# Moving the stores of one layer to the scalar engine's queue, and reordering the work at the border between two layers

## The chip, the cores and the metric

The kernel runs on one NeuronCore of a Trainium2 chip. The core has a matrix engine (PE; its weight loads are listed as PEld), a vector engine (DVE), a scalar engine (ACT), GpSimd (POOL) and a sync engine (SP) that here does nothing but issue DMAs. The metric is the device time of one execution in microseconds. The kernel before takes 1653.34 us, the median of three runs from 1653.21 to 1654.24.

## The reference

Attention within chunks of 64 positions feeds a two-layer chain of feed-forward blocks. Inputs are 64-bit floats that the kernel converts itself.

```python
scores = scale * np.matmul(q_c, k_c.transpose(0, 1, 2, 4, 3))        # 8 x 8 heads, 576 positions, chunks of 64
attn   = softmax(scores);  out = np.matmul(attn, v_c)
x  = out.transpose(0, 2, 1, 3).reshape(4608, 512)
h1 = x @ w_in1;  g1 = np.maximum(h1, 0) + alpha * np.minimum(h1, 0);  y = g1 @ w_out1     # 512 -> 2048 -> 512
h2 = y @ w_in2;  g2 = h2 - np.tanh(h2);                               out = g2 @ w_out2
```

## The kernel before

Each float32 operand of a large product is split into two parts, `hi` and `lo` (`hi` is the value rounded to a shorter mantissa, `lo` the rest), and a product is three matmuls: hi by hi, lo by hi, hi by lo. The 4608 tokens are nine blocks of 512.

**Layer one, blocks 0 to 6.** `step_one` does one of 16 feed-forward slices of a block: `up` (12 matmuls into a bank `hps`), then the `down` of the slice two steps earlier (12 matmuls into four banks `y`), then `act_g` (ACT reads `hps` as `neg` and `g`). At the last slice of a block (or half block) `done()` empties the four `y` banks: `put_bank` copies a bank to a stage tile `yst` on ACT (L642) and issues its store to `ysc` or `half` (L643) on SP. There are three stage tiles (`neg` and `xst` take turns in the same three), so the fourth bank's copy waits until the first store has landed. The next block's `down` starts a bank at a time and needs that bank emptied. Attention runs beside it, a tile of 128 tokens at a time: loads of `raw` (32 small DMAs of q and k for a pair of tiles, L340), `att_a` (DVE transposes them into `qt` and `ktc`, L385), `att_s` (scores on PE, L400), and so on; for tiles of the last two blocks `att_x_out` copies the result to a stage tile `xst` and issues its store to `xsc` (L536) on SP.

**Parked weights.** Beside this, second-layer weights are formed and written back to DRAM. `park_load` fetches 64-bit words into `desk[0]` (`rw`), `park_form` converts them (`to_f32_a`: two ACT instructions, L115 and L118; `to_f32_b`: four DVE instructions) into `desk[2]` (`mr`), `park_split` writes `hi` into `desk[1]` (`whi`, ACT L254) and `lo` (POOL L255), `park_store` issues both stores (L266). For a piece of kind `d`, the words and later `lo` lie in the same half of `mr`.

**Pairs of blocks.** From `two_blocks` on, two blocks go through together with a seven-product scheme on sums and differences of their operands. Pair s=0 is layer one on blocks 7 and 8, pairs s=1 to 4 are layer two, and `small` does the ninth block. `cycle(s, p)` is one of eight rounds of a pair; it issues products p1, p5, p6, p2, p3, p7, p4 (six matmuls each, L1200) and in between, as `gaps` says, matmuls of the output side (`downs`, L1107). PE reads a bank that `copy` (ACT, L1210) or `add` (DVE, L1207) prepared: p6 needs `copy(H0, X)` done, p3 needs `add(H1, X, p5)` done. `border(s)` hangs the preparation of the next pair's operands on named places of the rounds: `tokens` is a difference of two blocks (DVE, L710), `put` splits one into hi (ACT, L698) and lo (DVE, L700). `on(s, p, place, ...)` puts a call behind that place of round p.

Each engine runs its instructions in the order in which they were written, whatever waits ahead of them; the program's order decides what stands in SP's queue before what. Every DMA also signals one of eight completion counters (`DMAHW0` to `DMAHW7`), which are given out in turn over all DMAs of the program; a DMA first waits until the one eight before it has landed.

Of the kernel before, what the change touches and what calls it, by code (L numbers as in the profile page):

```python
# [11 lines left out]
I32 = mybir.dt.int32  # L12
# [15 lines left out]
def kernel(  # L28
# [19 lines left out]
    nc = tc.nc  # L48
# [3 lines left out]
    P = 128  # L52
# [148 lines left out]
    def park_load(kind, n, c):  # L201
# [7 lines left out]
            )  # L209
        parked[kind, n, c] = raw  # L210

    def park_form(kind, n, c):

        if kind == "u1":
            mr = desk[1]
            quarters = mr[:, 0:4].rearrange("p (g e) m -> p g e m", e=2)
            for e in range(2):
                hi, lo = (
                    wsplit[2 * n + e, 0][:, i].bitcast(F32).rearrange("p (g c m) -> p g c m", g=2, c=2)[:, :, c]
                    for i in range(2)  # L220
                )
                nc.gpsimd.tensor_tensor(out=quarters[:, :, e], in0=hi, in1=lo, op=ALU.add)
            sums = ((3, 1, 3, ALU.add), (1, 0, 1, ALU.subtract), (0, 3, 0, ALU.subtract), (2, 2, 0, ALU.subtract))
        else:
            mr = desk[2]
            flat = mr.rearrange("p s m -> p (s m)")
            to_f32_b([to_f32_a(parked[kind, n, c], flat[:, :512], flat.bitcast(I32)[:, 512:])])
            sums = ((4, 1, 3, ALU.add), (1, 0, 1, ALU.subtract), (5, 4, 0, ALU.subtract), (6, 2, 5, ALU.subtract))
        for o, x, y, op in sums if kind != "d" else ():
            nc.gpsimd.tensor_tensor(out=mr[:, o], in0=mr[:, x], in1=mr[:, y], op=op)  # L230
        parked[kind, n, c] = mr

    def park_split(kind, n, c):
# [2 lines left out]
        hi = desk[1].bitcast(F32R)  # L236
        if kind == "d":
            wd2[n] = dram.tile([P, 2, 4, P], F32, name=f"wd2_{n}")
            m, h, lo = mr[:, 0:4], hi[:, 0:4], mr[:, 4:8]
            to = [wd2[n][:, i] for i in range(2)]  # L240
        else:
            layer = 0 if kind == "u1" else 1
            if (layer, n) not in wu:
                wu[layer, n] = dram.tile([P, 7, 2, 2, P], F32, name=f"wu{layer}_{n}")
            if layer == 0:
                m, h, lo = mr[:, 0:4], hi[:, 4:8], mr[:, 0:4]
                to = [wu[0, n][:, 0:4, i, c] for i in range(2)]
            else:
                m, h, lo = mr[:, 0:7], hi[:, 0:7], mr[:, 0:7]
                to = [wu[1, n][:, :, i, c] for i in range(2)]  # L250
# [277 lines left out]
    def att_x_out(t):  # L528
# [4 lines left out]
        nc.scalar.activation(  # L533
            out=st.rearrange("p h (c d) -> p c h d", c=2), in_=xps.pop(t), func=AF.Copy
        )
        nc.sync.dma_start(out=xsc[j].rearrange("kk p t -> p kk t")[:, :, o:o + P], in_=st)  # L536


    def up(f, x, n, cols=None, hp=None):
# [97 lines left out]
    def put_bank(a, to, last=False):  # L637
        st = stage.tile([P, 512], F32, tag="st", name="yst")
        if last:
            nc.vector.tensor_copy(st, a)  # L640
        else:
            nc.scalar.activation(out=st, in_=a, func=AF.Copy)  # L642
        nc.sync.dma_start(out=to, in_=st)  # L643

    def finish_half(j, acc):
        spill[j] = dram.tile([KD, P, NB], F32, name=f"half{j}")
# [511 lines left out]
    def two_blocks(queue):  # L1158
# [91 lines left out]
        def parks_done():  # L1250
            spare.append(tuple(wide.tile([P, 2, 512], F32R, tag="w", name="xo") for _ in range(2)))
            new_slots(wide.tile([P, 2, 512], F32, tag="r", name="slots", bufs=1))
            raw["e1"] = [att.tile([P, NB], F32, tag=tag, name="e1") for tag in ("p", "pt")]
            raw["e2"] = [vpool.tile([P, NB], F32, tag="v", name="e2") for _ in range(2)]

        def border(s):
            m = s + 1
            if s == 0:
                on(s, 5, "p1", load_y, m, "b11", "b12")
                on(s, 6, "p1", load_y, m, "b22", "b21")  # L1260
                on(s, 6, "end", parks_done)
                on(s, 6, "end", turn, m)
                for p, place, fn, args in (
                    (6, "end", put, ("p1", "b11", V)), (6, "end", tokens, ("b11", "b12", "b11", V)),
                    (6, "end", tokens, ("b12", "b22", "b12", V)),
                    (7, "p6", put, ("p5", "b11", V)), (7, "p6", tokens, ("e1", "b22", "b11", V)),
                    (7, "p7", put, ("p6", "e1", V)), (7, "p7", tokens, ("e2", "b21", "e1", V)),
                    (7, "p4", put, ("p2", "b21", V)), (7, "end", put, ("p3", "b22", V)),
                    (7, "end", put, ("p7", "b12", V)), (7, "end", put, ("p4", "e2", V)),
                ):  # L1270
                    on(s, p, place, fn, m, *args)
                on(s, 7, "p7", drop, "b11")
                on(s, 7, "end", drop, "b21", "b22", "b12")
                on(s, 7, "end", lambda: [raw.pop(name) for name in ("e1", "e2")])
                return
            on(s, 4, "p1", load_y, m, "b11", "b12")
# [5 lines left out]
            on(s, 6, "end", tokens, m, "e1", "b22", "b11", V)  # L1282
            on(s, 6, "end", tokens, m, "e2", "b21", "e1", V)
            for p, place, product_, name in (
                (7, "p1", "p5", "b11"), (7, "end", "p6", "e1"), (7, "end", "p2", "b21"), (7, "end", "p3", "b22"),
                (8, "p6", "p7", "b12"), (8, "p6", "p4", "e2"),
            ):
                on(s + p // 8, p % 8, place, put, m, product_, name, V)
# [11 lines left out]
        for i, f in enumerate(range(DP, KF)):  # L1300
            p, form, split, later, store, latest, load = slips[i % 3]
            p += 2 * (i // 3)
            on(0, p, form, park_form, "d", f, 0)
            on(0, p + later, split, park_split, "d", f, 0)
            on(0, p + latest, store, park_store, "d", f, 0)
# [180 lines left out]
```

## Time and profile before

| | |
|---|---|
| median of three runs | 1653.34 us |
| the profiled execution | 1653.51 us, of which the span is 1651.5 us |
| PE busy | 1608.0 us (97%), 9309 matmuls |
| DVE busy | 1218.6 us (74%) |
| ACT busy | 989.2 us (60%) |
| POOL busy | 452.0 us (27%) |
| mean granted clock of PE | 0.99 |

All times in the rows are microseconds from the start of the span. A line number such as L643 is a line of the kernel before. A busy share says little here: PE is busy nearly all the time, so the time is its matmuls plus the few places where it stands still, and those are listed one by one in the view of waits. PE's granted clock is 1.00 or 0.50 of full speed (2.4 and 1.2 GHz).

### The profile page before, as it was taken

The numbers are of one execution on the slowest core, as the hardware profiler recorded it, in microseconds if no ns is written. First come the engines' busy times: TensorE is split into PE (matmuls) and PEld (weight loads), VectorE is DVE, ScalarE is ACT, GpSimd is POOL, SyncE is SP. The second block draws the span as 40 slices with busy tenths as digits, with TensorE's granted clock in tenths as the row PEclk, the third lists the DMA queues.
The fourth block names the chain that finished last, engine by engine and source line by source line (L and its number), as shares of the span: only waits on it lengthen the run. The fifth ranks groups of instructions, "written<-read, shape, count | busy, mean of one in ns | idle before, by whom it ended". The sixth has DMA issues, their size and how long they took to land. (4 is left out here: it accounts for less than half of the span.)

```text
span 1651.5 us, 26382 instructions
## 1 busy us (share of the span) xinstructions
PE 1608.0 (97%) x9309; PEld 1326.2 (80%) x9309; DVE 1218.6 (74%) x1864; ACT 989.2 (60%) x1769; POOL 452.0 (27%) x418
## 2 busy tenths in 40 slices
PE   7899999989989999999999999999999999999999
PEld 6678878877878887887778888888888888888887
DVE  7868957766768786674578688868886988688663
ACT  5657544554545554666557576757675767576553
POOL 1000001424435344323222222222222232223334
PEclk9899999999999999999999999999999999999999
DMA  9551334564656666648768764655465546545650
GB/s 255 167 189 48 90 78 114 122 170 118 162 130 155 157 166 182 211 139 282 271 207 289 256 211 136 192 161 175 141 191 165 168 147 185 161 145 171 206 160 26
DMA packets 339299, 276.49 MB, mean 167 GB/s; under 512 B 180432, under 2 KB 244960, under 8 KB 339168
## 3 DMA queue, kind: packets, MB, share of 16 engines
q1 hardware_dynamic: 339168, 274.82, 55.7%
q8 instruction: 73, 1.20, 0.3%
q14 instruction: 58, 0.48, 0.1%
HBM read 192.95 MB, written 81.79 MB: 166 GB/s over the span
## 5 line engine op out<-in xcount | busy, mean ns | idle before, releaser
L578 POOL TENSOR_TENSOR glo<-arena,ghi 128x512 fp32r<-128x512 f32 x147 | 206.4, 1419 | 505.7 <-ACT ghi L575 355.2
L547 PE MATMUL hps<-x,w 128*128 128x512 f32 (+1 forms) x1356 | 331.6, 394 | 5.9 <-ACT kt L374 5.3
L547 PEld LDWEIGHTS hps<-x,w 128*128 128x128 f32 x1356 | 257.6, 192 | 60.3 <-ACT kt L374 5.8
L1107 PE MATMUL y<-w,ghi 128*128 128x512 f32 x1152 | 296.2, 389 | 0.0
L1107 PEld LDWEIGHTS y<-w,ghi 128*128 128x128 f32 x1152 | 214.7, 188 | 43.4
L617 PE MATMUL y<-ghi,w 128*128 128x512 f32 x880 | 233.8, 399 | 6.2 <-ACT yst L642 6.2
L1200 PE MATMUL hpb<-w,wu 128*128 128x512 f32 (+1 forms) x888 | 205.3, 374 | 5.5 <-DVE hpb L1207 4.8
L1200 PE MATMUL hps<-w,wu 128*128 128x512 f32 (+1 forms) x888 | 205.1, 375 | 1.5 <-ACT hpb L1210 1.4
L617 PEld LDWEIGHTS y<-ghi,w 128*128 128x128 f32 x880 | 163.5, 190 | 42.2 <-ACT yst L642 7.1
L1200 PEld LDWEIGHTS hpb<-w,wu 128*128 128x128 f32 x888 | 158.7, 189 | 37.9 <-DVE hpb L1207 6.5
L1200 PEld LDWEIGHTS hps<-w,wu 128*128 128x128 f32 x888 | 158.8, 189 | 34.7 <-ACT hpb L1210 4.8
L1107 PE MATMUL y<-w,glo 128*128 128x512 f32 x576 | 163.0, 389 | 0.0
L560 DVE SCALAR_TENSOR_TENSOR g<-neg,nalpha_sb,g 128x512 f32<-128x512 f32 x112 | 90.8, 811 | 78.6 <-ACT g L559 78.4
L558 ACT ACTIVATE neg<-hps 128x512 f32<-128x512 f32 x112 | 66.5, 594 | 116.5 <-PE hps L547 116.3
L617 PE MATMUL y<-glo,w 128*128 128x512 f32 x440 | 126.4, 390 | 0.0
L1107 PEld LDWEIGHTS y<-w,glo 128*128 128x128 f32 x576 | 107.7, 188 | 22.2
L578 DVE TENSOR_TENSOR glo<-g,ghi 128x512 fp32r<-128x512 f32 x111 | 93.9, 846 | 35.9 <-ACT ghi L575 34.8
L575 ACT ACTIVATE ghi<-g 128x512 fp32r<-128x512 f32 x112 | 70.7, 631 | 70.2 <-DVE g L560 70.0
L607 DVE SCALAR_TENSOR_TENSOR arena<-sq,arena 128x512 f32<-128x512 f32 x119 | 103.0, 865 | 4.1
L599 ACT ACTIVATE w<-sq,bias_sb 128x512 f32<-128x512 f32 x144 | 104.0, 723 | 0.0
L602 ACT ACTIVATE ktc<-sq,edge_sb 128x512 f32<-128x512 f32 x144 | 103.8, 721 | 0.0
L608 DVE COPY_PREDICATED arena<-ktc,th 128x512 f32<-128x512 uint32 x119 | 93.2, 783 | 10.5 <-ACT th L591 0.5
(179 smaller groups left out, 2431.3 us busy)
## 6 DMA issues: line engine op xcount, KB each, us to landing
wu<-wu SPq DMA_DIRECT2D x336, 256.0 KB, 3.3
g<-arena SPq DMA_DIRECT2D x66, 256.0 KB, 3.6
arena<-g SPq DMA_DIRECT2D x65, 256.0 KB, 3.8
raww<-in_moe_w_in_dram SPq DMA_DIRECT2D x16, 512.0 KB, 5.4
v<-in_v_dram SPq DMA_DIRECT2D x32, 256.0 KB, 3.9
raww<-in_moe_w_out_dram SPq DMA_DIRECT2D x16, 512.0 KB, 5.4
rw<-in_moe_w_in_dram SPq DMA_DIRECT2D x16, 512.0 KB, 5.5
wu<-whi SPq DMA_DIRECT2D x32, 256.0 KB, 2.9
```

The source lines that it names most:

```text
L547: nc.tensor.matmul(out=hp[:, cols], lhsT=w[:, a, m], rhs=x[b][:, kk, cols], start=(kk == 0 and i == 0), stop=(kk == KD - 1 and i == 2),)
L558: nc.scalar.activation(out=neg, in_=hp, func=AF.Relu, scale=-1.0)
L560: nc.vector.scalar_tensor_tensor(out=g, in0=neg, scalar=nalpha_sb[:, f:f + 1], in1=g, op0=ALU.mult, op1=ALU.add)
L575: nc.scalar.activation(out=hi, in_=g, func=AF.Copy)
L578: lo_engine.tensor_tensor(out=lo, in0=g, in1=hi.bitcast(F32), op=ALU.subtract)
L599: nc.scalar.activation(out=self.w, in_=self.sq, func=AF.Square, bias=bias_sb)
L602: nc.scalar.activation(out=self.mask, in_=self.sq, func=AF.Relu, bias=edge_sb)
L607: nc.vector.scalar_tensor_tensor(out=g, in0=self.sq, scalar=TS[0], in1=g, op0=ALU.add, op1=ALU.mult)
L608: nc.vector.copy_predicated(g, self.mask.bitcast(U32), self.th)
L617: nc.tensor.matmul(out=acc[t], lhsT=lhsT, rhs=rhs, start=(f == ends[0] and i == 0), stop=(f == ends[1] and i == 2))
L1107: nc.tensor.matmul(out=self.acc[t], lhsT=lhsT, rhs=rhs, start=(self.f == self.ends[0] and i == 0), stop=(self.f == self.ends[1] and i == 2),)
L1200: nc.tensor.matmul(out=o, lhsT=w[:, a, c], rhs=x[c][:, b, :h], start=start and i == 0 and c == 0, stop=i == 2 and c == 1, skip_group_check ...
```

## The change

Five edits. (1) The stores of `put_bank` and of `att_x_out` are issued by ACT instead of SP: 24 and 8 DMAs. (2) For three of the parked pieces of s=0 (those whose form stands at the end of rounds 0, 2 and 4) the two ACT instructions of `to_f32_a` move ahead, to the place `p4` of the same round. (3) `lo` of a `d` piece goes to the second half of `desk[1]` instead of the half of `mr` that held the words. (4) At the border of s=0 the differences come first and go to tiles of the attention (`extras`, three `tokens` at the end of round 6), and the tiles that the parked weights leave, the turn of the operand tiles and all seven `put` come later (from round 7's p6 to round 0 of the next pair). (5) At the borders of the other pairs the `put` of p5 moves from behind p1 of round 7 to behind p6.

```diff
+    def park_words(kind, n, c):
+        flat = desk[2].rearrange("p s m -> p (s m)")
+        parked[kind, n, c] = to_f32_a(parked[kind, n, c], flat[:, :512], flat.bitcast(I32)[:, 512:])
...
-            to_f32_b([to_f32_a(parked[kind, n, c], flat[:, :512], flat.bitcast(I32)[:, 512:])])
+            if not isinstance(parked[kind, n, c], tuple):
+                park_words(kind, n, c)
+            to_f32_b([parked[kind, n, c]])
...
-            m, h, lo = mr[:, 0:4], hi[:, 0:4], mr[:, 4:8]
+            m, h, lo = mr[:, 0:4], hi[:, 0:4], desk[1][:, 4:8]
...
-        nc.sync.dma_start(out=xsc[j].rearrange("kk p t -> p kk t")[:, :, o:o + P], in_=st)
+        nc.scalar.dma_start(out=xsc[j].rearrange("kk p t -> p kk t")[:, :, o:o + P], in_=st)
...
-        nc.sync.dma_start(out=to, in_=st)
+        nc.scalar.dma_start(out=to, in_=st)
...
+                on(s, 6, "p1", extras)
+                on(s, 6, "end", tokens, m, "e1", "b12", "b11", V)
+                on(s, 6, "end", tokens, m, "b12", "b22", "b12", V)
+                on(s, 6, "end", tokens, m, "e2", "b22", "e1", V)
+                on(s, 7, "p6", parks_done)
+                on(s, 7, "p6", turn, m)
                 for p, place, fn, args in (
-                    (6, "end", put, ("p1", "b11", V)), (6, "end", tokens, ("b11", "b12", "b11", V)),
-                    (6, "end", tokens, ("b12", "b22", "b12", V)),
-                    (7, "p6", put, ("p5", "b11", V)), (7, "p6", tokens, ("e1", "b22", "b11", V)),
-                    (7, "p7", put, ("p6", "e1", V)), (7, "p7", tokens, ("e2", "b21", "e1", V)),
+                    (7, "p6", put, ("p1", "b11", V)), (7, "p6", tokens, ("b11", "b21", "e2", V)),
+                    (7, "p7", put, ("p5", "e1", V)), (7, "p4", put, ("p6", "e2", V)),
                     (7, "p4", put, ("p2", "b21", V)), (7, "end", put, ("p3", "b22", V)),
-                    (7, "end", put, ("p7", "b12", V)), (7, "end", put, ("p4", "e2", V)),
+                    (8, "p6", put, ("p7", "b12", V)), (8, "p6", put, ("p4", "b11", V)),
...
-                (7, "p1", "p5", "b11"), (7, "end", "p6", "e1"), (7, "end", "p2", "b21"), (7, "end", "p3", "b22"),
+                (7, "p6", "p5", "b11"), (7, "end", "p6", "e1"), (7, "end", "p2", "b21"), (7, "end", "p3", "b22"),
...
+            if form == "end":
+                on(0, p, "p4", park_words, "d", f, 0)
```

Three places of the program's order follow, each before and after. The line numbers of the kernel after are 5 to 11 higher.

On SP, before, the four stores of block 2 (`ysc2`) stand behind raw loads, parked weights, a `v` load and a load of words. The name in the brackets is what the DMA waits for.

```order
L340 DMA raw_3410<-in_k_dram 32x8x32 [waits DMAHW4_49]
L266 DMA wu1_1_3617<-whi_2784 896x1x128 [waits DMAHW5_49,Activation_49]
L266 DMA wu1_1_3617<-mr_2785 896x1x128 [waits DMAHW6_49,DVE_49,Pool_49]
L301 DMA v_3625<-in_v_dram 128x8x64 [waits DMAHW7_49,PE_49]
L206 DMA rw_2783<-in_moe2_w_in_dram 128x2x256 [waits DMAHW0_49]
L643 DMA ysc2_3694<-yst_3695 128x512 [waits DMAHW1_49,Activation_49]
L643 DMA ysc2_3694<-yst_3698 128x512 [waits DMAHW2_49,Activation_49]
L643 DMA ysc2_3694<-yst_3701 128x512 [waits DMAHW3_49,Activation_49]
L643 DMA ysc2_3694<-yst_3704 128x512 [waits DMAHW4_49,Activation_49]
```

A store is issued only when all that stands above it has been issued. On ACT, after, the same four stores stand between the copies that fill their tiles.

```order
L647 ACTIVATE yst_3695<-y0_2668 128x512 [waits PE_49]
L648 DMA ysc2_3694<-yst_3695 128x512 [waits DMAHW1_49,Activation_49]
L647 ACTIVATE yst_3698<-y1_2669 128x512 [waits PE_49]
L648 DMA ysc2_3694<-yst_3698 128x512 [waits DMAHW2_49,Activation_49]
L647 ACTIVATE yst_3701<-y2_2670 128x512 [waits DVE_49,PE_49]
L648 DMA ysc2_3694<-yst_3701 128x512 [waits DMAHW3_49,Activation_49]
L647 ACTIVATE yst_3704<-y3_2671 128x512 [waits DMAHW1_49,PE_49]
L648 DMA ysc2_3694<-yst_3704 128x512 [waits DMAHW5_49,Activation_49]
```

Each copy but the first now stands behind a store, and each store behind the counter of an older DMA, mostly one of SP's.

On SP, after, at the end of block 5: the loads of the pairs' first operands (`arena`) are followed at once by the first ring of weights (`wu`), since the stores of `ysc5` that stood between them are gone.

```order
L698 DMA arena_6846<-xsc7_3515 128x512 [waits DMAHW1_49,PE_49]
L698 DMA arena_6846<-xsc7_3515 128x512 [waits DMAHW2_49]
L698 DMA arena_6846<-xsc7_3515 128x512 [waits DMAHW3_49]
L698 DMA arena_6846<-xsc7_3515 128x512 [waits DMAHW4_49]
L287 DMA wu_6955<-wu0_0_2905 128x512 [waits DMAHW5_49,PE_49]
L287 DMA wu_6955<-wu0_0_2905 128x512 [waits DMAHW6_49]
L287 DMA wu_6958<-wu0_0_2905 128x512 [waits DMAHW7_49,PE_49]
L287 DMA wu_6958<-wu0_0_2905 128x512 [waits DMAHW0_49]
```

The four stores of `ysc5`, now on ACT, wait for counters 1, 3, 5 and 7: the first and third `arena` load and the first and third `wu` load of these rows.

On DVE, before, at the end of round 6 and in round 7 of s=0 (L700 is the lo of a `put`, L710 a difference, L1207 the `add` that PE's p3 needs):

```order
L1154 SCALAR_TENSOR_TENSOR arena<-neg,nalpha_sb,arena 128x512 x4
L700 TENSOR_TENSOR xo<-arena,xo 128x512 x2
L710 TENSOR_TENSOR arena<-slot,arena 128x512
L710 TENSOR_TENSOR arena<-arena 128x512
L710 TENSOR_TENSOR slot<-arena,slot 128x512
L710 TENSOR_TENSOR arena<-arena 128x512
L1207 TENSOR_TENSOR hpb<-hps,ptb 128x512
```

The same place after:

```order
L1159 SCALAR_TENSOR_TENSOR arena<-neg,nalpha_sb,arena 128x512 x4
L715 TENSOR_TENSOR e_8424<-slot,arena 128x512
L715 TENSOR_TENSOR e_8425<-arena 128x512
L715 TENSOR_TENSOR slot<-arena,slot 128x512
L715 TENSOR_TENSOR arena<-arena 128x512
L715 TENSOR_TENSOR e_8426<-arena,e_8424 128x512
L715 TENSOR_TENSOR e_8427<-arena,e_8425 128x512
L1212 TENSOR_TENSOR hpb<-hps,ptb 128x512
L705 TENSOR_TENSOR xo<-arena,xo 128x512 x2
```

The two lo of the first `put`, which wait for ACT's hi, moved behind the `add`; six differences stand ahead of it.

## Rows read from the trace of the kernel before

**Rows 1.** Who PE waited for: total us, times, longest us.
```profile
PE y L617 <- ACT yst L642: 6.2, 2, 4.2
...
PE hpb L1200 <- DVE hpb L1207: 4.8, 4, 2.4
PE sc L400 <- DVE ktc L385: 4.8, 1, 4.8
...
PE hps L1200 <- ACT hpb L1210: 1.4, 3, 0.5
...
PE hpb L1200 <- ACT hps L1210: 0.6, 1, 0.6
```
**Rows 2.** Stretches: length, each engine's busy time (instructions), PE clock, DMA share, GB/s.
```profile
355.87:361.57 5.70, 5.70 (x13) 4.45 (x14) 3.39 (x6) 4.73 (x10) 0.00 (x0) 0.50 0.44 142
361.57:367.27 5.70, 5.70 (x26) 4.70 (x25) 5.43 (x11) 2.84 (x5) 0.00 (x0) 1.00 0.31 82
484.41:487.86 3.45, 3.45 (x68) 3.04 (x69) 3.37 (x6) 2.90 (x7) 3.14 (x5) 0.51 0.98 262
...
846.25:849.67 3.42, 3.42 (x10) 2.67 (x9) 1.68 (x3) 1.65 (x4) 0.00 (x0) 0.50 0.14 31
345.00:348.00 3.00, 3.00 (x15) 2.48 (x14) 2.88 (x8) 1.69 (x3) 0.00 (x0) 1.00 0.39 64
...
652.00:654.00 2.00, 1.56 (x7) 0.94 (x6) 0.00 (x0) 0.00 (x0) 0.00 (x0) 1.00 1.06 407
```
**Rows 3.** Timeline of ACT, end of block 2: start, us, instruction [idle before <-releaser].
```profile
355.22 0.60 ACT L642 ACTIVATE yst<-y 128x512 f32<-128x512 f32 x1 [8.36 <-DMA ysc<-yst]
```
**Rows 4.** Timeline of SP's issues, end of block 2.
```profile
341.02 5.72 SPq L340 DMA_DIRECT2D raw<-in_k_dram  x10
...
350.07 6.10 SPq L643 DMA_DIRECT2D ysc<-yst  x4
```
**Rows 5.** DMA issues by kind: count, KB each, median us to landing.
```profile
raw<-in_k_dram SPq DMA_DIRECT2D x192, 32.0 KB, 2.0
...
half<-yst SPq DMA_DIRECT2D x8, 256.0 KB, 2.2
```
**Rows 6.** One line, L643 on SP: issue time in ns, min/median/max, first and last start.
```profile
L643 SPq DMA_DIRECT2D ysc<-yst x16: 319/349/1242, 350.1 to 655.6; - x16
```
**Rows 7.** Timeline of SP's issues, end of block 3.
```profile
450.82 1.51 SPq L206 DMA_DIRECT2D rw<-in_moe_w_in_dram  x1
453.96 3.74 SPq L643 DMA_DIRECT2D ysc<-yst  x4
457.79 8.98 SPq L340 DMA_DIRECT2D raw<-in_q_dram  x16
...
475.25 5.65 SPq L266 DMA_DIRECT2D wu<-whi  x3
```
**Rows 8.** Timeline of ACT, after block 3.
```profile
479.40 0.95 ACT L254 ACTIVATE whi<-mr 128x896 fp32r<-128x896 f32 x1 [7.95 <-DMA wu<-whi]
```
**Rows 9.** Timeline of SP's issues, end of block 5.
```profile
645.92 2.54 SPq L693 DMA_DIRECT2D arena<-xsc  x4
```
**Rows 10.** Timelines of PE and of ACT, end of block 5.
```profile
655.59 0.73 PE L617 MATMUL y<-ghi,w 128*128 128x512 f32 x2 [2.03 <-ACT yst L642]
...
654.94 0.60 ACT L642 ACTIVATE yst<-y 128x512 f32<-128x512 f32 x1 [6.19 <-DMA ysc<-yst]
```
**Rows 11.** Timeline of ACT, s=0: words of a parked piece, end of round 5.
```profile
820.70 0.67 ACT L118 ACTIVATE mr<-rw 128x512 int32<-128x512 uint32 x1 [6.18 <-DMA wd<-mr]
```
**Rows 12.** Timeline of DVE, s=0, start of round 7.
```profile
839.65 0.69 DVE L700 TENSOR_TENSOR xo<-arena,xo 128x512 fp32r<-128x512 f32 x1 [2.88 <-ACT xo L698]
...
841.46 1.79 DVE L710 TENSOR_TENSOR slot<-arena,slot 128x512 f32<-128x512 f32 x1
...
844.85 0.69 DVE L1207 TENSOR_TENSOR hpb<-hps,ptb 128x512 f32<-128x512 f32 x1
```
**Rows 13.** Timeline of DVE, s=1, start of round 7.
```profile
1004.36 1.30 DVE L700 TENSOR_TENSOR xo<-arena,xo 128x512 fp32r<-128x512 f32 x2
```

More of the change, by code (lines that the diff above doesn't have):

```diff
@@ L225, in park_form @@
             mr = desk[2]
-            flat = mr.rearrange("p s m -> p (s m)")
-            to_f32_b([to_f32_a(parked[kind, n, c], flat[:, :512], flat.bitcast(I32)[:, 512:])])
+            if not isinstance(parked[kind, n, c], tuple):
+                park_words(kind, n, c)
+            to_f32_b([parked[kind, n, c]])
             sums = ((4, 1, 3, ALU.add), (1, 0, 1, ALU.subtract), (5, 4, 0, ALU.subtract), (6, 2, 5, ALU.subtract))
@@ L1252, in parks_done, with extras @@
             new_slots(wide.tile([P, 2, 512], F32, tag="r", name="slots", bufs=1))
+        def extras():
             raw["e1"] = [att.tile([P, NB], F32, tag=tag, name="e1") for tag in ("p", "pt")]
@@ L1260, in border @@
                 on(s, 6, "p1", load_y, m, "b22", "b21")
-                on(s, 6, "end", parks_done)
-                on(s, 6, "end", turn, m)
+                on(s, 6, "p1", extras)
[4 more added lines that the diff above has]
+                on(s, 7, "p6", turn, m)
                 for p, place, fn, args in (
-                    (6, "end", put, ("p1", "b11", V)), (6, "end", tokens, ("b11", "b12", "b11", V)),
-                    (6, "end", tokens, ("b12", "b22", "b12", V)),
-                    (7, "p6", put, ("p5", "b11", V)), (7, "p6", tokens, ("e1", "b22", "b11", V)),
-                    (7, "p7", put, ("p6", "e1", V)), (7, "p7", tokens, ("e2", "b21", "e1", V)),
+                    (7, "p6", put, ("p1", "b11", V)), (7, "p6", tokens, ("b11", "b21", "e2", V)),
+                    (7, "p7", put, ("p5", "e1", V)), (7, "p4", put, ("p6", "e2", V)),
                     (7, "p4", put, ("p2", "b21", V)), (7, "end", put, ("p3", "b22", V)),
-                    (7, "end", put, ("p7", "b12", V)), (7, "end", put, ("p4", "e2", V)),
+                    (8, "p6", put, ("p7", "b12", V)), (8, "p6", put, ("p4", "b11", V)),
                 ):
-                    on(s, p, place, fn, m, *args)
-                on(s, 7, "p7", drop, "b11")
-                on(s, 7, "end", drop, "b21", "b22", "b12")
+                    on(s + p // 8, p % 8, place, fn, m, *args)
+                on(s, 7, "end", drop, "b21", "b22")
+                on(s + 1, 0, "p6", drop, "b12", "b11")
                 on(s, 7, "end", lambda: [raw.pop(name) for name in ("e1", "e2")])
```

## The prediction

> **What bounds the kernel now.** Read the page's busy shares first and lay them aside: PE has work for nearly the whole span, so a change can win only where PE stands still or runs at its lower clock. The second view is PE's list of waits [rows 1]. Four entries of it lie where the change does something: 6.2 us on ACT's copies of the `y` banks, in two pieces of 4.2 and 2.0; 4.8 us on DVE's `add`, one of 2.4 and, with four in all, three of 0.8; one of 4.8 us on DVE's transposes into `ktc`; and 1.4 and 0.6 us on ACT's `copy`. The rest (the first 100 us, a tile of attention at 394 us) has nothing to do with the edits. The third view is the stretch behind the three longest of these stops: the granted clock is 0.50, and 5.70 us then hold 13 matmuls where the next 5.70 us hold 26 [rows 2]. So these three stops, of 4.2, 4.8 and 2.4 us, are paid for twice. The last views are the timelines of the engine that was waited for, which show what it waited for itself.
>
> **Part 1, the stores of layer one.** Block 2: ACT stood 8.36 us, from 346.9 us on, before its copy of the fourth bank, waiting for the first store to land [rows 3]. That store was issued at 350.07, because ten raw loads from 341.02 on and four more DMAs stood ahead of it on SP [rows 4]. From ACT it would wait only for its counter, number 1, which the seventh raw load used (the tenth uses number 4 in the order shown). With ten issues in 5.72 us that load goes out near 344.5 and, at the median of 2.0 us, lands near 346.5. The store then lands at about 349.1 (an issue of 0.35 and 2.2 us, the median of the `half` stores [rows 5]), the fourth copy ends by 350, and PE wants that bank at 355.87 less 4.2, some 351.6. The 4.2 us go, and with them the low clock: 13 matmuls of 5.70/26 = 0.22 us, 2.8 us.
>
> Block 3: SP issued its stores from 453.96 and only then 32 raw loads from 457.79; the store of `whi` behind them went out at 475.25 [rows 7], ACT's next write of `whi` waited 7.95 us for it and ran at 479.40 [rows 8], and behind it on ACT and DVE came the transposes that PE waited 4.8 us for. Without stores between, SP starts the raw loads when PE has read the buffer; the load of words ahead of them was issued by 450.82 + 1.51 = 452.3, over five us before 457.79 [rows 7]. So the stop of 4.8 us goes as well; with it goes half of the 3.45 us at clock 0.51 at most, 1.7 us, of which I take 1.2, since most of those 68 instructions are short attention matmuls.
>
> Block 5 is where the edit does not help. Its stores take counters behind `arena` and `wu` loads. The four `arena` loads went out from 645.92 to 648.5, and the first store, issued behind them, had landed only when ACT's wait ended at 654.94 [rows 9, 10], some 6.3 us after its issue; so, at the same delay, the first `arena` load lands near 645.9 + 6.3 = 652.2, with the DMA engines busy all the time (share 1.06 [rows 2]). Only then may ACT issue its first store, and the other three copies now stand behind it, 0.6 us each with an issue of 0.35 between: from 652.6 the last would end at 655.2 if nothing else held it, and it also waits for the first store to land and for the counters of the `wu` loads. I put it near 656, against 655.54 now; PE wanted that bank at 655.59 - 2.03 = 653.6 [rows 10], and it now waits for the second and third bank as well. PE's 2.0 us stay and become about 3.0: I charge 1.0. It could be minus 2.0 (the stop gone), and plus 5 if ACT stands until a `wu` load lands some us later and the clock drops too.
>
> The new instructions: 32 DMA issues on ACT. No trace here shows one on ACT; on SP such an issue takes 319 to 1242 ns, median 349 [rows 6]. At the median four of them make 1.4 us at each of the six places, at the longest 5 us; at best nothing. What hides them is ACT's idle time there and the round of `down` between `act_g` and the next use of `hps`. I take the median and cost nothing beyond block 5; without that cover, the longest would cost up to 3 us at three of the places, which goes into the range. What is queued behind a waiting store on ACT is the next copy, the four `ptb` copies, the next `ghi` and the next `neg`; PE waits for the second and third of these about one slice later.
>
> **Part 2, parked words and `lo`.** ACT's L118 waited 6.18 us for the store of the previous `lo` at 820.70 [rows 11], since both use one half of `mr`; with `lo` elsewhere this wait has no cause. PE's stops before p6 are the 1.4 and 0.6 of [rows 1]: small stops in which ACT came late to `copy` behind L118 or behind a hi of `xo`, which moves away in part 3. The longest piece, 0.5, I leave in place: it is in round 1, where the moved instructions trade places with copies of `y` banks that ACT has to do anyway, unless the words land earlier. The other 0.8 and the 0.6 go: 1.4. Bounds: 0, if ACT now stands at the new place until the words land, and 2.0.
>
> **Part 3, border of s=0.** DVE lost 2.88 us between the two lo of `put` p1, then did four differences, two of which took 1.79 us, so that `add` ran from 844.85 to 845.54 [rows 12]; PE stood 2.4 us, so it wanted `add` at 843.1, or 842.6 without the 0.5 us stop just before. After, six differences start where the first lo had started, at 839.65 - 2.88 - 0.69 = 836.1. At 0.69 to 0.9 us each they end between 840.2 and 841.5, and `add` by 842.2 at the latest. The 2.4 us go, and with them most of half of 3.42 us at clock 0.50 [rows 2], 1.7; I take 1.4. Late next would be the product p7 of the following pair, whose `put` now stands in its own round: DVE needs 0.69 for `add` and four lo, 3.5 us, while PE does twelve `downs` and two products, 24 matmuls of 0.22 or 5.3 us. That leaves about 2 us.
>
> **Part 4, borders of s=1 to 3.** Two lo, 1.30 us together, stood between the six differences and `add` [rows 13]; without them `add` can start 1.2 us earlier, against a stop of 0.8. All three go: 2.4 us. The operand has a whole round until its product.
>
> **Sum.** Stops: 4.2 + 4.8 + 1.4 + 2.4 + 2.4 = 15.2. Clock: 2.8 + 1.2 + 1.4 = 5.4. Block 5: minus 1.0. Net 19.6. The profiled execution took 1653.5, of which the span is 1651.5, and lies 0.2 above the median: 1653.5 - 19.6 = 1633.9, say 1634.
>
> **The Trainium skill against this.** On block 2 the rows show a wait for a place in a queue: the DMA share is 0.39 between 345 and 348 us [rows 2], just when the store could go. The Trainium skill, "DMA: Bandwidth & Descriptors", section "Issuing engines are not separate DMA queues", says that DMAs from all engines interleave on the same 16 DMA engines, and that issuing from several engines saves only the time of issue. By that rule block 2 would win four issues of 0.35 us, 1.4 us, and the sum would be some 1639 to 1640. The trace agrees with it at block 5 and not at block 2.
>
> **Rivals.**
> *The 16 DMA engines are the limit.* The first store of block 2 lands late whoever issues it, since the words' load and the parked stores are in flight. Against it: the share of 0.39. It keeps 4.2 + 2.8 us: 1634 + 7 = 1641. Chance 10%.
> *The raw loads of block 3 stay late.* They now share counters with ACT's stores, so SP may wait for ACT, and the words' load ahead of them is slow. If less than 4.8 us are won, up to 6 us stay: 1640. Chance 12%.
> *Block 5 gets better.* If the first store lands early among the `wu` loads, its 2.0 us go as well: 1631. Chance 10%.
> *The difference does nothing for `add`.* If DVE needs 0.9 us for every one of the six and more, as in the slow pair of [rows 12], `add` is late by 1 to 2 us and keeps half of part 3: 1636. That lies inside the likeliest case's own range.
> *Slower.* ACT stands in its stores' waits: each waits for an older DMA, most of them SP's, and `act_g` is behind it. If blocks 3, 4, 5 and the half blocks each cost PE what block 2 costs now, 4.2 + 2.8 = 7 us, five of them make 35 us against 20 won: 1669. It decides from the third such block on, where the gain is used up. For it speaks that every store in the order shown carries such a wait; against it, block 2 as worked out above, where the counter comes free 2 us after the copy and the fourth bank still comes over 1 us early. Chance 4%.
>
> **Chances.** The likeliest case, 1630 to 1639, has 62%; the three rivals above 32% (two to 1641, one to 1631); slower 4%; 2% for anything else. The range that holds the time 8 times in 10 is 1628 to 1643. What a measurement of this kernel can tell from no change is about 0.2%, 3.3 us. Faster by more than that, below 1650: 92%; within it: 4%; slower: 4%.
>
> **What would show it.** In the list of PE's waits after: no wait of 4 us for `yst` and none for `ktc` near 480; the `y` wait at block 5 still there; no wait of more than 0.2 us for `add`; one of about 0.5 us left for `copy`, in round 1 of s=0. The clock at 0.50 should be gone behind these places. SP's raw loads of block 3 should start near 452. It is wrong if ACT shows waits of several us on its stores at more than block 5, or if the gain of layer one is below 8 us.

## The result, and the profile after

The changed kernel takes 1634.8 us, the median of four runs from 1633.25 to 1636.59, against 1653.5 for the kernel before, timed beside it (1653.21 to 1654.24). The ratio is 0.9887, with an interval from 0.9869 to 0.9904. The profiled execution took 1636.59 us, of which the span is 1634.5. The prediction was 1634 in a range from 1628 to 1643.

The list of PE's waits answers to [rows 1]. Line numbers in traces of the changed kernel are 5 higher in layer one and at the places of the pairs that are spoken of here. These are the waits that have to do with the change:

```profile
PE y L622 <- ACT yst L647: 4.4, 4, 2.0
PE hpb L1205 <- DVE hpb L1212: 1.0, 1, 1.0
PE y L1112 <- POOL glo L583: 0.9, 1, 0.9
PE sc L405 <- DVE ktc L390: 0.8, 1, 0.8
```

The wait for `yst` is shorter in sum (4.4 for 6.2) but there are four pieces instead of two; the one for `ktc` has shrunk to 0.8 and the four for `add` have become one of 1.0; those for `copy` are gone; a wait on POOL is new.

PE's clock behind the stops, the same view as [rows 2]: behind block 2, behind the transposes of block 3, behind the `add` of round 1 and in the border of s=0, and last at block 5.

```profile
348.00:353.70 5.70, 5.70 (x27) 1.00 1.08 346
474.00:480.00 6.00, 6.00 (x28) 1.00 0.48 90
740.00:745.00 5.00, 4.23 (x19) 1.00 0.99 329
828.00:834.00 6.00, 6.00 (x28) 1.00 0.85 265
640.50:646.20 5.70, 3.72 (x9) 0.50 1.10 365
```

Of the three places that had 0.50 before, none is left; block 5, which had 1.00, now has 0.50.

**Block 2.** ACT's timeline, where [rows 3] showed the wait of 8.36 us in front of the fourth copy:

```profile
343.33 0.37 ACTq L648 DMA_DIRECT2D ysc<-yst  x1
343.74 0.60 ACT L647 ACTIVATE yst<-y 128x512 f32<-128x512 f32 x1 [1.65 <-PE y L622]
344.37 0.33 ACTq L648 DMA_DIRECT2D ysc<-yst  x1
344.80 0.60 ACT L647 ACTIVATE yst<-y 128x512 f32<-128x512 f32 x1 [0.46 <-DVE p L437]
345.43 0.33 ACTq L648 DMA_DIRECT2D ysc<-yst  x1
345.86 0.60 ACT L647 ACTIVATE yst<-y 128x512 f32<-128x512 f32 x1 [0.46 <-DMA ysc<-yst]
```

An issue takes ACT 0.33 to 0.37 us. The first store, issued at 343.33, has landed when the fourth copy begins at 345.86; that copy ends at 346.46, and PE does not wait for it.

**Block 3.** SP's timeline, which answers to [rows 7]:

```profile
439.60 0.67 SPq L206 DMA_DIRECT2D rw<-in_moe_w_in_dram  x1
440.61 11.44 SPq L345 DMA_DIRECT2D raw<-in_q_dram  x16
452.10 9.11 SPq L345 DMA_DIRECT2D raw<-in_k_dram  x16
461.80 5.75 SPq L271 DMA_DIRECT2D wu<-whi  x3
```

The matmuls around this place run 10.5 us earlier than before, so 440.61 corresponds to 451.1 in the trace of before, where these loads began at 457.79. But the 32 loads now take 20.6 us to issue (11.44 + 9.11), and the store of `whi` behind them comes late enough to hold ACT for 3.82 us (7.95 in [rows 8]). The copies of the same block wait on SP's DMAs:

```profile
445.30 0.60 ACT L647 ACTIVATE yst<-y 128x512 f32<-128x512 f32 x1 [1.89 <-DMA wu<-mr]
447.24 0.60 ACT L647 ACTIVATE yst<-y 128x512 f32<-128x512 f32 x1 [1.34 <-DMA raw<-in_q_dram]
466.04 0.95 ACT L259 ACTIVATE whi<-mr 128x896 fp32r<-128x896 f32 x1 [3.82 <-DMA wu<-whi]
```

PE stops there for 0.50 and 0.09 us, which it did not before.

**Block 5**, ACT's timeline again (before, [rows 10]):

```profile
631.98 0.60 ACT L647 ACTIVATE yst<-y 128x512 f32<-128x512 f32 x1 [0.90 <-PE y L622]
637.93 0.34 ACTq L648 DMA_DIRECT2D ysc<-yst  x1
638.31 0.60 ACT L647 ACTIVATE yst<-y 128x512 f32<-128x512 f32 x1 [5.73 <-DMA arena<-xsc]
639.66 0.60 ACT L647 ACTIVATE yst<-y 128x512 f32<-128x512 f32 x1 [0.75 <-DMA arena<-xsc]
643.22 0.60 ACT L647 ACTIVATE yst<-y 128x512 f32<-128x512 f32 x1 [2.96 <-DMA ysc<-yst]
```

The first store is ready at 632.6 and issued at 637.93, when the first `arena` load, issued by SP at 631.87, has landed. The wait is printed on the copy behind the store, since issuing instructions are not counted. PE stops for 1.57, 0.37 and 1.98 us, at the banks of the last three copies.

**Border of s=0**, DVE's timeline (before, [rows 12]): the six differences run without a gap, at 0.6 us from start to start, and `add` now waits for PE.

```profile
824.54 0.69 DVE L715 TENSOR_TENSOR e<-slot,arena 128x512 f32<-128x512 f32 x1
826.94 1.29 DVE L715 TENSOR_TENSOR e<-arena,e 128x512 f32<-128x512 f32 x2
829.57 0.70 DVE L1212 TENSOR_TENSOR hpb<-hps,ptb 128x512 f32<-128x512 f32 x1 [1.34 <-PE hps L1205]
```

**A ledger.** All kernels told of here run the same 9309 matmuls in one order, so two traces can be compared matmul by matmul. The table gives by how many us each stretch became shorter (minus) or longer against the trace of before. It is worked out from the starts of single matmuls; the boundaries are at 343, 371, 504, 693, 842 and 906 us of before. `lo_only`, `words_only`, `border0_only` and `without_edit5` were run once each; the kernel before, run once beside them, took 1648.31 us, 5 us less than the median of its first three runs. Except for the 13 us of `words_only`, their total times therefore decide nothing of the size that is asked here, and the table is read in their place.

| trace | start | block 2 | block 3 | block 5 | rounds of s=0 | border s=0 | rest | sum |
|---|---|---|---|---|---|---|---|---|
| predicted | 0 | -7.0 | -6.0 | +1.0 | -1.4 | -3.8 | -2.4 | -19.6 |
| after | -3.4 | -7.2 | -4.3 | +4.7 | -2.2 | -4.3 | -0.4 | -17.0 |
| after_again | -1.2 | -7.2 | -5.8 | +5.0 | -2.3 | -4.3 | -2.6 | -18.4 |
| before_again | -4.0 | -0.7 | +1.4 | +1.5 | 0.0 | 0.0 | 0.0 | -1.8 |
| stores_only | -3.8 | -7.2 | -4.0 | +4.5 | +1.1 | -1.6 | -0.1 | -11.0 |
| lo_only | -3.4 | -0.4 | +1.7 | +1.8 | -2.5 | -1.6 | +0.2 | -4.3 |
| words_only | -3.3 | +0.1 | +1.1 | +1.5 | +11.5 | -2.9 | +0.2 | +8.2 |
| border0_only | -4.4 | -0.5 | +1.0 | +1.6 | -0.5 | -4.3 | +0.3 | -6.8 |
| without_edit5 | -3.9 | -7.2 | -5.9 | +5.1 | -2.3 | -4.2 | +0.2 | -18.2 |
| b5_on_sp | -2.8 | -7.2 | -4.2 | +0.6 | -1.7 | -4.3 | -0.9 | -20.5 |
| b5_one_load | -3.3 | -7.2 | -5.4 | +4.4 | -2.3 | -4.3 | -2.2 | -20.3 |
| b5_moved | -1.3 | -7.2 | -5.4 | -2.3 | -2.4 | -4.3 | -1.7 | -24.5 |
| moved_no_words | -2.5 | -7.2 | -4.5 | -2.3 | -2.8 | -4.3 | -2.5 | -26.1 |

### The profile page after: what moved, and what is told of

Its sections match the earlier page's. It is cut to its first block, busy times and chain, and to the rows that moved or that the text cites. A ratio compares the mean times of both kernels' runs of the same rounds, so it can differ in the third digit from the quotient of the medians.

```text
span 1634.5 us, 26370 instructions
## 1 busy us (share of the span) xinstructions
PE 1603.2 (98%) x9309; PEld 1322.1 (81%) x9309; DVE 1226.1 (75%) x1864; ACT 989.8 (61%) x1769; POOL 453.6 (28%) x418
## 4 chain that ended last, share of the span: by engine, by line
PE 89%; DVE 3%; DMA 2%; SPq 2%; issue 2%; ACT 1%; POOL 1%; DVEq 0%; ACTq 0%; POOLq 0%
PE y L1112 28%; PE y L622 17%; PE hps L552 17%; PE hps L1205 12%; PE hpb L1205 12%; PE sc L405 1%; PE sc L476 1%; POOL glo L583 1%; SPq L345 1%; SPq L311 1%; DMA rw<-in_moe_w_in_dram 0%; DMA arena<-xsc 0%; DMA wu<-whi 0%; DVE wm L134 0%; DVE wm L138 0%
## 5 line engine op out<-in xcount | busy, mean ns | idle before, releaser
L583 POOL TENSOR_TENSOR glo<-arena,ghi 128x512 fp32r<-128x512 f32 x139 | 195.2, 1417 | 483.4 <-ACT ghi L580 367.4
L226 POOL TENSOR_TENSOR whi<-w 128x256 f32<-128x256 f32 x32 | 25.9, 831 | 264.3 <-DVE g L565 230.6
L612 DVE SCALAR_TENSOR_TENSOR arena<-sq,arena 128x512 f32<-128x512 f32 x111 | 95.6, 861 | 3.8
```

The costliest lines, as they stand in the source:

```text
L583: lo_engine.tensor_tensor(out=lo, in0=g, in1=hi.bitcast(F32), op=ALU.subtract)
L612: nc.vector.scalar_tensor_tensor(out=g, in0=self.sq, scalar=TS[0], in1=g, op0=ALU.add, op1=ALU.mult)
```

## The experiments

**1. `stores_only`: edit 1 on the kernel before.**

```diff
-        nc.sync.dma_start(out=xsc[j].rearrange("kk p t -> p kk t")[:, :, o:o + P], in_=st)
+        nc.scalar.dma_start(out=xsc[j].rearrange("kk p t -> p kk t")[:, :, o:o + P], in_=st)
...
-        nc.sync.dma_start(out=to, in_=st)
+        nc.scalar.dma_start(out=to, in_=st)
```

> The kernel before with edit 1 alone: the stores of emptied banks and of attention results issued by ACT, nothing else. The measure is the start of the same PE matmul in two traces, since all these kernels run the same 9309 matmuls in one order. In the changed kernel, matmuls started 3.4 us earlier before block 2, 10.5 earlier behind it, 14.8 behind block 3 and only 10.1 behind block 5. Theory (the stores' place in the queue and the older DMA whose counter they take are all that edit 1 changes): the same steps here, minus 7.1 at block 2, minus 4.3 at block 3, plus 4.7 at block 5, and nothing behind, so 6.7 us without the 3.4 of the start: a time near 1646.5. Rival (part of these steps comes from the other edits, which also shift the parked weights' DMAs): a step that differs by over 1 us. The 3.4 us before block 2: if they belong to edit 1 they are here again and the time is 1643; if they are chance of the run, the start may come out anywhere between the two.

Measured: 1643.15 us (1641.65 to 1647.16), ratio 0.9943 with an interval from 0.9929 to 0.9956. The three steps of layer one are those of the changed kernel within 0.3 us, so they belong to edit 1 alone, and the start is early here too. Behind layer one, where nothing was expected, the stops for `copy` grew by 1.1 us and the border of s=0 lost 1.6 less; `lo_only` shows the same 1.6 without any edit there, so this is how much the low clock behind that `add` differs between executions.

**2. `b5_on_sp`: block 5's stores back on SP.**

```diff
+        on_sp[0] = j == LB - 2
...
-        nc.scalar.dma_start(out=to, in_=st)
+        (nc.sync if on_sp[0] else nc.scalar).dma_start(out=to, in_=st)
```

> The changed kernel, with the four stores of block 5 alone issued by SP again. In the changed kernel ACT stood 5.73 us in front of its second copy, until the first arena load had landed, and PE stood 1.57, 0.37 and 1.98 us for the banks, with the clock at 0.50 behind it. Theory (ACT's stores wait for the arena and wu loads whose counters they take): back to one stop of 2.0 us for the fourth bank and no low clock, 4.7 us won, near 1630. Rival (the arena and wu loads fill the DMA engines, share 1.10 from 640 to 646 us, so that the stores and the wait come late whoever issues them): stops at the second and third bank stay, time within 1 us of 1634.8.

Measured: 1634.22 us (1632.34 to 1637.16), ratio 0.9887 (0.9873 to 0.9900). One stop is left, 2.63 us for the fourth bank, and no low clock: the step at block 5 is +0.6 instead of +4.7, so 4.1 us are won at the place where 4.7 were expected. The stop that is left doesn't come from ACT's waits: the first store, issued by SP at 634.87 behind the same loads, ends ACT's wait for it only at 641.35, 6.5 us later (L648 is the line of the copy in this kernel).

```profile
PE y L622 <- ACT yst L648: 2.6, 1, 2.6
641.35 0.60 ACT L648 ACTIVATE yst<-y 128x512 f32<-128x512 f32 x1 [6.78 <-DMA ysc<-yst]
```

The median doesn't show the 4.1 us; it lies only 0.6 below the changed kernel's, while the runs of either spread over 3 us and more.

**3. `b5_one_load`: the same bytes, other counters.**

```diff
-    at(end - KF + 1, load_y, 0, "b11", "b21")
...
+        nc.sync.dma_start(out=arenas[0][:, 0:KD], in_=xsc[n1 - 2].rearrange("kk p t -> p kk t"))
...
+    at(end - KF + 1, load_y_at_once, 0, "b11", "b21")
```

> The changed kernel, with the four arena loads in front of block 5's stores made into one DMA of the same 1 MB. The same bytes are in flight at the same time, but the counters shift: the first two stores, still on ACT, now take the counters of older DMAs (a parked store, the load of words), the third that of the first wu load. Theory (counters): ACT's wait of 5.73 us in front of the second copy goes, PE's stops of 1.57 and 0.37 us for the second and third bank too; for the fourth bank, whose copy waits until the first store has landed, between 0 and 2.0 us are left: 4.7 to 6.7 us won, 1628 to 1630. Rival (engines full of the same bytes): the stops stay, 1634.8 within 1 us.

Measured: 1634.21 us (1632.44 to 1639.45), ratio 0.9891 (0.9876 to 0.9905); the step at block 5 is +4.4. So the time that the theory expected was not won. ACT's timeline says why:

```profile
630.97 0.60 ACT L647 ACTIVATE yst<-y 128x512 f32<-128x512 f32 x1 [0.90 <-PE y L622]
632.40 0.34 ACTq L648 DMA_DIRECT2D ysc<-yst  x1
632.79 0.60 ACT L647 ACTIVATE yst<-y 128x512 f32<-128x512 f32 x1 [1.21 <-DMA wu<-mr]
636.98 0.60 ACT L647 ACTIVATE yst<-y 128x512 f32<-128x512 f32 x1 [3.59 <-DMA rw<-in_moe_w_in_dram]
640.97 0.60 ACT L647 ACTIVATE yst<-y 128x512 f32<-128x512 f32 x1 [3.40 <-DMA wu<-wu]
```

The first store now goes out at 632.40, not 637.93, with the same 1 MB of loads in flight. The second waits for the load of words and the third for the first `wu` load: the three DMAs named as their counters. So the wait of 5.73 us was the counter's. But the step did not change, and for that there are two reasons. Other counters took its place: the load of words, issued at 630.27, took six us to land as well, although I had named it and taken it for free by then. And the store itself was slow. From issue to landing the first store of block 5 took 5.2 us in the changed kernel and 7.6 us here, where it was issued 5.5 us earlier; the first store of block 2 in the changed kernel took 2.1. In this order, and behind them PE's row for the fourth bank:

```profile
DMA to landing us min/median/max: 5.2/5.2/5.2
DMA to landing us min/median/max: 7.6/7.6/7.6
DMA to landing us min/median/max: 2.1/2.1/2.1
641.62 1.22 PE L622 MATMUL y<-ghi,w 128*128 128x512 f32 x2 [3.03 <-ACT yst L647]
```

It landed at 640.0, and the fourth copy, which needs its tile, could not end before 640.6. PE wanted that bank at 641.62 - 3.03 = 638.6 (the last row). So about 2 us of the stop of 3.03 would be left without any counter: an estimate from these rows. The theory holds for the first wait, and the rival, the loads that are in flight, for most of the last stop.

**4. `b5_moved`: the `arena` loads and the first rings issued behind block 5's stores.**

```diff
-    at(end - KF + 1, load_y, 0, "b11", "b21")
-    at(end - KF + 2, lambda: [ring_slots(home(f"s{i}", [P, 2, 2, 2, P], F32R, "wu")) for i in range(2)])
+    at(end - KF + 4, load_y, 0, "b11", "b21")
+    at(end - KF + 4, lambda: [ring_slots(home(f"s{i}", [P, 2, 2, 2, P], F32R, "wu")) for i in range(2)])
```

> The changed kernel, with the four arena loads three slices later and the first two rings of wu two slices later, so that neither is in flight when block 5's stores are issued. Theory (counters) and rival (DMA engines) both expect no stop at block 5, 6.7 us won, 1628; it is the bound of what block 5 can give. It could lose part of it if the operands of the first product, which are formed from the arena loads one slice behind their new place, come late: then a stop appears on the matmuls of block 6 or the stop moves to the transfer into the pairs.

Measured: 1629.09 us (1626.93 to 1629.52), ratio 0.9851 (0.9838 to 0.9865): below the changed kernel, whose interval begins at 0.9869. ACT's timeline of block 5:

```profile
633.57 0.34 ACTq L648 DMA_DIRECT2D ysc<-yst  x1
634.59 0.34 ACTq L648 DMA_DIRECT2D ysc<-yst  x1
635.65 0.33 ACTq L648 DMA_DIRECT2D ysc<-yst  x1
638.02 0.60 ACT L647 ACTIVATE yst<-y 128x512 f32<-128x512 f32 x1 [2.39 <-DMA ysc<-yst]
```

Three stores go out as their copies end, the fourth copy comes in time, and PE does not stop. The step is -2.3 instead of +4.7. No operand of the pairs came late. The first store lands 4.4 us after its issue here. Since theory and rival expected the same of this kernel, it bounds what the place is worth and does not choose between them: with the loads gone, the waits for their counters and the slow landing behind them went together.

**5. `lo_only`: edit 3 on the kernel before.**

```diff
-            m, h, lo = mr[:, 0:4], hi[:, 0:4], mr[:, 4:8]
+            m, h, lo = mr[:, 0:4], hi[:, 0:4], desk[1][:, 4:8]
```

> The kernel before with edit 3 alone: lo of a parked piece goes to a half of another tile than the words. Read by the starts of the same PE matmul. Theory (L118's waits for the store of lo, 22.7 us over seven times, are edit 3's, and where the two ACT instructions stand is edit 2's): the stop before p6 at 824.4 (0.64 us, behind a wait of 6.18) goes, the one at 747.5 (0.54, L115 and L118 without a wait right ahead of the copy) stays: minus 0.6 to 1.0 in all behind round 6. Rival (the place of the words decides everywhere): no stop changes by over 0.2. A second question is the start: its code is that of the kernel before, so a start that is 1 to 4 us earlier here shows that the 3.4 us before block 2 are chance.

Measured, one execution: 1649.37 us. Of the stops for `copy` only the one in round 1 is left, as expected, but all the others went, not just the one of 0.6, and the step is -2.5. By the starts of the matmuls, the listed stops of 0.14, 0.32, 0.64 and 0.51 were worth 0.43, 0.60, 0.93 and 0.49 us. The start is 3.4 us earlier although its code is that of before.

```profile
PE hps L1200 <- ACT hpb L1210: 0.5, 1, 0.5
```

**6. `words_only`: edit 2 on the kernel before.**

```diff
...
+            if form == "end":
+                on(0, p, "p4", park_words, "d", f, 0)
```

> The kernel before with edit 2 alone: for three pieces L115 and L118 move ahead to the place p4, and lo still shares a half with the words. Theory: the stop at 747.5 (0.54) goes and the add of round 1 is late instead by 1.0, as in the changed kernel, since ACT now waits at the new place until the words land and what DVE does ahead of the add starts later; the stop at 824.4 stays or grows. In sum between minus 0.3 and plus 1.0. Rival (the late add of round 1 comes from edit 4 or 1): no stop for add in round 1.

Measured, one execution: 1661.68 us, and +11.5 us in the rounds. The expectation failed. PE's waits there:

```profile
PE hps L1205 <- ACT hpb L1215: 5.5, 3, 3.2
PE hpb L1205 <- DVE hpb L1212: 5.4, 6, 1.0
PE hpb L1205 <- ACT hps L1215: 2.5, 1, 2.5
```

L118 still waits for the store of lo (2.91 us in round 1), and now does so in front of four copies of `y` banks and both Relus of a slice. Edit 2 costs 11 us without edit 3; beside it, it is worth nothing: the rounds win 2.5 us with edit 3 alone and 1.7 to 2.4 in six traces with both.

**7. `border0_only`: edit 4 on the kernel before.** The edit is the part of the change's diff that concerns `s == 0` in `border`, with `extras`.

> The kernel before with edit 4 alone: the border of s=0 in its new order. Theory: the stop of 2.42 us for add and the 1.6 us of low clock behind it go, as in the changed kernel, and the 0.51 stop for copy just before stays, since L118's wait is still there: minus 4.0 to 4.4. Rival (the new order needs ACT free of the parked weights' waits, so edits 2 and 3): add is late by 1 us or more and the clock still falls: minus 2 or less.

Measured, one execution: 1647.91 us; the step at the border is -4.3, the same as in every trace with edit 4, so it needs none of the other edits. The 0.51 for `copy` ahead of it went too, which was not expected.

**8. `without_edit5`: the changed kernel with the `put` of p5 behind p1 again.**

```diff
-                (7, "p6", "p5", "b11"), (7, "end", "p6", "e1"), (7, "end", "p2", "b21"), (7, "end", "p3", "b22"),
+                (7, "p1", "p5", "b11"), (7, "end", "p6", "e1"), (7, "end", "p2", "b21"), (7, "end", "p3", "b22"),
```

> The changed kernel without edit 5: at the borders of s=1 to 3 the put of p5 is behind p1 of round 7 again. Theory (edit 5 takes the 0.8 us stops for add away, and the lo instructions that it moves stand one after another on DVE while POOL makes a glo, which took 3.90 us there instead of 1.3 and kept PE 0.93): the three stops of 0.8 come back and the stops for glo go; between the border of s=0 and the end the difference to the kernel before changes by 0 within 0.3, against minus 0.35 in the changed kernel. Rival (the stops for glo come with edit 4, which left other tiles to the pairs): stops for glo of the same size stay, and the end is about 2 us later than in the changed kernel.

Measured, one execution: 1635.43 us. The three stops for `add` are back (0.81, 0.78, 0.78), no stop for `glo` is left, and the rest changes by +0.2: as the theory said. With edit 5 the rest was -0.4, -2.6, -0.9, -2.2, -1.7 and -2.5 in six traces, so with edit 5 this stretch won 1.7 us on average of the 2.4 that the stops for `add` held; where the stop for `glo` was 0.93, most of it was given back there.

**9 to 11. `moved_no_words`, `after_again`, `before_again`.** The first is number 4 without edit 2; the others are the two kernels unchanged.

```diff
-            if form == "end":
-                on(0, p, "p4", park_words, "d", f, 0)
```

> The changed kernel with the arena loads three and the first rings two slices later, and without edit 2: the words are converted where they were. From the runs so far: with edit 3 alone the rounds 1 to 6 of s=0 won 2.5 us, with both edits 2.25, so leaving edit 2 out should bring 0.3 us, a stop of 0.5 for copy in round 1 in place of 1.0 for add. Theory: 1628.5 to 1629, no difference in time that can be told from 1629.1 with edit 2, and 5 to 6 us below the changed kernel. Rival (the 5.7 us between 1634.8 and 1629.1 are the start's chance and not block 5): a time of 1632 or more, with the stop at block 5 gone.

> The changed kernel once more, to see what differs from one execution to the next at the same places: expected are 1633 to 1637, the stops of 1.6, 0.4 and 2.0 at block 5 and of 0.8 for ktc again within 0.3 us; the stops for glo at the borders, which were 0.93 at one border here and at another one in a second kernel with the same code there, should change their place; the start, up to 3 us either way.

> The kernel before once more, for its start. Nine traces of other kernels, three of them with the very code of the kernel before up to 330 us, started the matmuls near 96 us 1.3 to 4.3 us earlier than the trace of before did. If the start is chance of the execution, this trace can come out anywhere from 0 to 4 us earlier, and the time follows it; if it belongs to the build, it comes out at 0 again within 0.3.

Measured: `moved_no_words` 1628.77 us (1626.84 to 1633.58), ratio 0.9865 (0.9848 to 0.9882), the same as number 4 as far as can be told and below the changed kernel beside it; the late `add` of round 1 is gone and a stop of 0.55 for `copy` stands there, as expected. `after_again` 1635.33 us (1634.36 to 1639.42), ratio 0.9908 (0.9888 to 0.9928), with stops of 1.61, 0.40 and 2.42 at block 5 and 0.53 for `ktc`, all but the 2.42 within the 0.3 expected; of the stops for `glo` only 0.09 is left, at the border of s=2, where it had been 0.93: I had expected its place to change, and between the two traces of this kernel its size did instead (in `b5_on_sp`, with the same code there, the 0.93 stands at the border of s=1). `before_again` 1652.18 us (1649.5 to 1654.85): its trace starts 4.0 us earlier than the first trace of the same kernel. So the start is chance of the execution, and the trace that the prediction was read from has the latest start of all thirteen.

## Why the prediction was right, point by point

The time came out within 1 us, but not because every term was right, and partly by luck: between the two first traces the start alone gave 3.4 us. In the second measurement the changed kernel took 1635.33 beside 1651.62 for the kernel before, 16.3 us less and not 18.7. At the places named, the two first traces differ by 13.6 us (17.0 less the 3.4 of the start). With the second traces of both kernels the four possible pairs give 13.6, 15.9, 17.2 and 19.5, on average 16.6 against 19.6 predicted.

- *Block 2: right.* Predicted 7.0, measured 7.2 in each of the eight traces with edit 1, the stop and the low clock behind it. By the rule of the Trainium skill that was weighed there ("DMA: Bandwidth & Descriptors", section "Issuing engines are not separate DMA queues"), 1.4 us would have been won. What it leaves out is that the store's place among SP's own DMAs changes with the issuing engine.
- *Block 3: right in kind, short in size.* The raw loads start where predicted (451.1 for 452). I took their issue to last as long as before. It grew from 16.8 us (8.98 for q and 7.84 for k) to 20.6: SP's waits in that stretch are 1.3 us for the load of words just ahead of them, 1.0 for an older one of their own and 1.6 put down to PE, and none for a store of ACT's, which the rival had named first. So 0.8 us of the stop for `ktc` stayed; the banks of this block, where I charged nothing, stop PE for 0.6. Predicted 6.0, measured 4.3 and 5.8. The rival of raw loads that stay late set its limit at 4.8, so the first of these traces is its case, and the second is not.
- *Block 5: this term was mis-sized.* "I charge 1.0", with "plus 5 if ACT stands until a `wu` load lands some us later and the clock drops too". It cost 4.7. The working was right up to the wait: the first `arena` load lands 6.1 us after its issue (6.3 assumed). But the last copy, for which the first store must have landed, ends at 643.8, or 658.6 with the 14.8 us that matmuls were earlier up to here; I had put it near 656. The store took 5.2 us to land, where I had allowed about 3 (from 652.2, when ACT may issue it, to the start of a copy that ends at 656). The stops add up to 3.9 us where I took 3.0, and the clock fell, which the central value left out. Numbers 2 to 4 show where it comes from: the counters hold the first wait, and the loads themselves slow the store's landing. With those loads a few slices later the place wins 2.3 us, the 2.0 of the rival "block 5 gets better", though not for its reason. Part of the 4.7 is the trace it is counted from: against the four traces of the old stores that have the low clock there (+1.5 to +1.8) it is about 3.
- *Part 2: right for another reason than I gave in round 1.* Predicted 1.4, measured 2.2. The 0.5 that I left in place did go, and a late `add` of 1.0 took its place, since ACT now waits 1.44 us for the words there. Edit 3 carries all of this part.
- *Part 3: right.* Predicted 3.8, measured 4.3. The six differences take 0.6 us each from start to start; the rival with 0.9 did not come. The share of the clock in it is luck: behind the same stop of 2.4 the clock stayed at 1.00 in `stores_only` and `lo_only`, and against those the edit is worth 2.7.
- *Part 4: the stops for `add` go, as predicted (2.4), but part of it is given back.* POOL made one `glo` in 3.90 us while DVE did lo instructions of several `put` in a row, and PE waited 0.93 us. I had asked who waits for DVE, and not what POOL does beside it.
- *What would show it.* No `add` wait above 0.2: wrong (1.0, round 1). Copy's 0.5 in round 1: wrong. Clock gone behind the three places: right. "Wrong if the gain of layer one is below 8 us": it is 6.7 in the first pair of traces and 8.0, 9.0 and 10.3 in the other three, so that condition was met once of four. ACT stood long on its stores at block 5 alone; at block 3 1.9 us at most.
- *Not predicted: the start.* 3.4 us of the difference between the profiled executions come from before 97 us, where no edit reaches. They are in `before_again` too.

## What to carry to other kernels

A DMA moved to another engine's queue leaves the old queue's order, but not the completion counters; so list, for each moved DMA, the DMA whose counter it takes, all of them and not the first alone, and how long those take to land. It doesn't leave the other traffic either: behind 1 MB of loads and more a store took 5 to 7.6 us to land, from either engine. Where a large load is issued just ahead of a store on the critical path, move the load by a few slices, which takes away both: here that was worth more than 5 us with nothing lost. And an instruction that waits should not be moved ahead of others before its wait is gone: edit 2 alone cost 11 us, and after edit 3 it was not needed.

## What was not expected of the hardware

**The same stop, another clock.** PE's rows behind its stop at block 5, in three kernels: 2.03 us in the kernel before, 1.99 us in `border0_only`, 2.63 us in `b5_on_sp`. The columns are those of [rows 2], PE alone.

```profile
655.50:660.00 4.50, 4.41 (x19) 1.00 0.23 82
```

```profile
651.60:656.00 4.40, 4.27 (x12) 0.61 0.21 74
```

```profile
642.00:646.00 4.00, 4.00 (x17) 1.00 0.73 231
```

The clock fell behind the stop of 1.99 and not behind those of 2.03 and 2.63. So what a stop of about 2 us costs differs by 1.5 us from one execution to the next. Of six traces with SP's stores at block 5, four have the low clock; the two without it are the one that the prediction was read from and `b5_on_sp`.

**POOL beside DVE.** The timelines of POOL and of DVE in the changed kernel, at the border of s=2:

```profile
1172.23 3.90 POOL L583 TENSOR_TENSOR glo<-arena,ghi 128x512 fp32r<-128x512 f32 x1 [4.32 <-ACT ghi L580]
1180.03 1.30 POOL L583 TENSOR_TENSOR glo<-arena,ghi 128x512 fp32r<-128x512 f32 x1 [3.90 <-ACT ghi L580]
```

```profile
1171.31 1.29 DVE L705 TENSOR_TENSOR xo<-arena,xo 128x512 fp32r<-128x512 f32 x2
1172.50 1.90 DVE L705 TENSOR_TENSOR w<-arena,w 128x512 fp32r<-128x512 f32 x3
1174.31 0.69 DVE L705 TENSOR_TENSOR w<-slot,w 128x512 fp32r<-128x512 f32 x1
1174.91 0.70 DVE L1212 TENSOR_TENSOR hps<-hpb,ptb 128x512 f32<-128x512 f32 x1
1175.52 1.76 DVE L705 TENSOR_TENSOR w<-arena,w 128x512 fp32r<-128x512 f32 x2
```

The same instruction took POOL 1.30 us alone and 3.90 beside a run of DVE instructions that read two tiles each. Of these, two took 1.76 us together where two of the like take 1.29 just before; those ahead of them were not slower (1.90 us for three). The Trainium skill says so: "GPSIMD Engine Reference", section "1. Specifications", has POOL's interface to the tiles' memory shared with VectorE, with contention where an instruction of DVE has two inputs there. The trace agrees, with these numbers. The other traces bear it out: each of the six with edit 5 has a `glo` of 3.3 to 3.9 us, and none of the seven without it has one above 2.6, number 8 among them, where only the place of the `put` differs. That DVE's reads, and nothing else about that place, slow POOL was read from the timelines.
